# Gated mix of an FFT filter and a GELU unit on Trainium2: first loads through SyncE, last down products in single PSUM banks, other buffers and addresses for the GELU products

## The chip, the core and the metric

The kernel runs on one core of a Trainium2 chip. A core has a matrix engine (TensorE, PE in the profile; its weight loads are PEld), VectorE (DVE), ScalarE (ACT), GpSimd (POOL) and SyncE (SP), which here only issues transfers. Each engine works through its own instructions in the order in which they were recorded and waits on semaphores for what other engines and transfers produce. PE multiplies from on-chip memory (SBUF, 128 partitions) and writes into eight accumulation banks (PSUM), which DVE and ACT read. Transfers are issued by SP, POOL or ACT and carried by 16 DMA engines.

The metric is the device time of one execution in microseconds (us). Three executions of the kernel before took 1328.35 to 1328.8 us, with a median of 1328.49 us.

## What is computed

For x of 2048 tokens by 576 features, the kernel mixes a filter in frequency space with a GELU-gated unit, token by token:

```python
g = sigmoid((x * gate_w).sum(-1, keepdims=True))
X = rfft2(x, axes=(-2, -1)) * (w_r + 1j * w_i)
a = irfft2(X, s=(2048, 576), axes=(-2, -1))
b = (gelu(x @ w_gate, approximate=True) * (x @ w_up)) @ w_down     # 576 -> 4608 -> 576
return g * a + (1 - g) * b
```

## The kernel before, in words

**The gated unit fills PE.** The 4608 hidden features are 36 tiles of 128. Tokens are taken in two halves `p` of 1024, each in two blocks `tb` of 512. Every fp32 operand is split into a high and a low part (`xhi`/`xlo`, two halves of a `gub` or `dn` buffer), and a product is made of three: high by high, low by high, high by low. Hidden tiles come in pairs `i`. The first pairs of a half are made directly (`normal`, `chain`, lines L851 to L868), the rest in blocks of seven products instead of eight (`products`, `seven`, L1283 to L1389). Each pair leaves four results of 128x512, named `c11`, `c12` for block 0 and `c21`, `c22` for block 1. `finish` applies the GELU on ACT and multiplies on DVE, and `split_h` writes the result, split in two, to a hidden buffer that `take(wants)` picks from those free. From there the result is the stationary operand of the down products.

**The down products.** `down` (L958) makes a tile of 128 tokens by 576 outputs: for each of two hidden tiles (`part` 0 and 1) six products of 288 columns into a pair of PSUM banks (`ps_dn`, two such pairs in turn). ACT evicts it, scaled by 1 - g, into one of four buffers `stg`, and POOL adds that to `yd` in HBM. A block of `products` puts eight such tiles between its seven products.

**The hidden buffers.** Four of them, `base` = `hb0`, `hb1`, `hb2`, `hx`, serve the direct pairs and `c11`, `c12`; two more, `extra` = the second half of a `gub` buffer and `ext`, serve `c21`, `c22`. A buffer has 4096 bytes in a partition. Tiles are laid out in SBUF one after the other in the order in which `mk` names them, so a wider tile moves all that are named after it. In the built program the byte addresses, modulo 512, are: `hb0`, `hb1`, `hb2` and `ext` 448, the half of `gub` 384, `hx` 480, and `rows` (which also holds the operands of the column transform) 480. All `dn` buffers are at 384.

**The filter** is worked in the gaps between matmuls: DVE and ACT do the transforms along the rows, and PE does the column transform as 32 small products (`product`, L294) that stand between the others in the middle of the run.

**The start** (L1434 to L1471). `x0[k]` are the five tiles of x for the first 512 tokens, 256 KB each; `w0[:, k]` and `w1[:, k]` are the matching pieces of the first two gate/up weight tiles, 128 KB each. SP issues all of x and the weights of k = 0, POOL the other eight weight pieces. PE first does six idle products on a zeroed buffer, then `first_chains` (L870): for k = 0, 1, 2 six products for tile 0 and six for tile 1, then k = 4 and 3 of tile 0, then of tile 1. ACT makes the high part of each weight and x piece, DVE the low part, in the fixed order in which the loop records them. A transfer of SP takes one of eight semaphores in turn, and waits until the transfer eight places ahead of it has landed.

**The end** (`finale`, L1419). The last results are added and stored straight to y: four tiles with a whole pair of banks each, then four tiles whose part 0 is done for all of them before part 1. Of these, two sit in bank pairs (`pair()`), one in the two banks `px`, one in the two banks `pgu`. `down_last` (L999) makes the products, lets DVE add the tile to what was loaded (L1008, 576 columns for a whole tile, 288 for each half otherwise), and lets SP store it (L1012 or L1010).

Of the kernel before, what the change touches and what calls it, by code (L numbers as in the profile page):

```python
# [11 lines left out]
F32R = mybir.dt.float32r  # L12
# [7 lines left out]
KF = D // 2 + 1  # L20
# [3 lines left out]
HD = D // 2  # L24
KT = 5
TB = 512
SW = 2 * (KF + 1)
ROWS = 5120
UNIT = ROWS // 4
# [120 lines left out]
def _block_of_token():  # L150

    out = [0] * 16
    for o in range(16):
        out[4 * LEFT[o % 4] + LEFT[o // 4]] = o
    return out, [4 * TAKEN[o % 4] + TAKEN[o // 4] for o in out]
# [20 lines left out]
def _build(nc, tc, a):  # L176
    with ExitStack() as ctx:
# [3 lines left out]
        vec, act, pl, pe = nc.vector, nc.scalar, nc.gpsimd, nc.tensor  # L181

        def mk(n, shape, dt=F32):
            return pool.tile([P] + shape, dt, name=n, tag=n)

        def f(x):
            return x.bitcast(F32)
# [7 lines left out]
        _, loc = _block_of_token()  # L195
# [4 lines left out]
        low = mk("low", [5008])  # L200
        ext = mk("ext", [2 * TB])
        raw = [low[:, i * (KT * 256 + D):(i + 1) * (KT * 256 + D)] for i in range(2)]
        hb = [mk(f"hb{i}", [2, TB], F32R) for i in range(3)]
        gl = [mk(f"gl{i}", [TB]) for i in range(2)]
        xraw = mk("xraw", [4, TB])
        stg = [mk(f"stg{i}", [2, HD]) for i in range(4)]
        tmp = mk("tmp", [2 * UNIT + 112])
        sgn = tmp[:, 2 * UNIT + 112 - KF:]
        gs = mk("gs", [NB])
        gate = mk("gate", [NB])  # L210
        omg = mk("omg", [NB])
        msk = mk("msk", [2 + 96])
# [10 lines left out]
        def ps_gu():  # L223
            return psum.tile([P, TB], F32, name="pgu", tag="pgu", bufs=2)

        def ps_dn():
            return psum.tile([P, 2, 512], F32, name="pdn", tag="pdn", bufs=2)

        def ps_x(c):
            return psum.tile([P, TB], F32, name=f"px{c}", tag=f"px{c}", bufs=1)  # L230
# [3 lines left out]
        def ps_one():  # L234
            ones[0] += 1
            return ps_x(ones[0] % 2)

        def copy(o, i):
            act.activation(o, i, AF.Copy)  # L239
# [229 lines left out]
        def gu_at(j):  # L469
            return (j + (2 * FIRST[0] - 1) * (j >= NT)) % 3  # L470

        BLOCKS = []
        for p in range(2):
            y, z = (gu_at(NT * p + 2 * FIRST[p] - q) for q in (2, 1))
# [321 lines left out]
        def gu_of(j):  # L796
            return gub[gu_at(j)].rearrange("p (l t k) -> p l t k", l=2, t=KT)
# [13 lines left out]
        def seq(key, *steps):  # L811

            q = todo[key] = [fn for _, fn in steps]
            for n, _ in steps:
                at(n, lambda: q and q.pop(0)())
# [96 lines left out]
        base = list(hb) + [mk("hx", [2, TB], F32R)]  # L912
        extra = []
# [7 lines left out]
        def split_h(g, hold, wants=(), soon=False):  # L921

            def high():
                hold.append(take(wants))
                copy(hold[0][:, 0], g)

            def low():
                vec.tensor_tensor(hold[0][:, 1], g, f(hold[0][:, 0]), ALU.subtract)
                credit[0] -= 0.7

            return ((1, high), (2, low)) if soon else ((3, high), (5, low))

        def down_mm(ps, prev, t, part, apart=False):
            c = slice(t * P, (t + 1) * P)
            j, hold, key = prev[3][part]
            due(key)
            h = hold[0]
            due(("dn", j))
            d = dn[j % 4]
            steps = [(n, half) for n in range(3) for half in range(2)]  # L940
            for n, half in sorted(steps, key=lambda x: x[1]) if apart else steps:
                l, q = ((0, 0), (0, 1), (1, 0))[n]
                pe.matmul(ps[half], h[:, l, c], d[:, q, half * HD:(half + 1) * HD],  # L943
                          start=part == 0 and n == 0, stop=part == 1 and n == 2)
            tick(6 * 0.131)
# [44 lines left out]
        def rest(i):  # L990
            if i < 4:
                return stg[i].rearrange("p c k -> p (c k)")
            return low[:, D * (i - 4):D * (i - 3)]

        def load_last(tb):
            for i in range(4 * tb, 4 * tb + 4):
                nc.sync.dma_start(rest(i), yd[8 + i])

        def down_last(prev, t, v, part):  # L999

            i = 4 * prev[2] + t
            whole = len(v) == 1
            down_mm((v[0][:, 0, 0:HD], v[0][:, 1, 0:HD]) if whole else v, prev, t, part, not whole)
            if part == 1:
                o = rest(i).rearrange("p (c k) -> p c k", c=2)
                for c in range(1 if whole else 2):
                    oc, vc = (o, v[0][:, :, 0:HD]) if whole else (o[:, c], v[c])
                    vec.scalar_tensor_tensor(oc, vc, omg[:, 8 + i:9 + i], oc, op0=ALU.mult, op1=ALU.add)  # L1008
                    if not whole:
                        nc.sync.dma_start(a["y"][8 + i][:, c * HD:(c + 1) * HD], o[:, c])  # L1010
                if whole:
                    nc.sync.dma_start(a["y"][8 + i], rest(i))  # L1012

        def pair():
            return (ps_dn(),)
# [282 lines left out]
        def products(b, i):  # L1298

            p, j = b.p, b.p * NT + 2 * i  # L1300
# [4 lines left out]
            def finish(name, x, o):  # L1305
                g, v = x
                hold = made[name] = []

                def mult():
                    vec.tensor_tensor(o, o, v, ALU.mult)  # L1310
                    credit[0] -= 0.69

                def gelu():
                    act.activation(o, g, AF.Gelu_apprx_tanh)

                wants = extra if name in ("c21", "c22") else base
                if end and p and name in ("c21", "c12"):
                    gelu()
                    seq((name, p, i), (1, mult), *split_h(o, hold, wants, True))
                else:  # L1320
                    soon = 0 if end else 1
                    high, low = (fn for _, fn in split_h(o, hold, wants))
                    late = name in ("c22", "c12") and not (end and p)
                    seq((name, p, i), (1 + late, gelu), (2 + (soon if name != "c21" else 0) + late, mult), (4 + soon + late - end, high), (5 + 2 * soon + late, low))
# [16 lines left out]
            for n, (name, nd) in enumerate(zip(("a11", "a12", "s2", "s3", "s1", "a22", "s4"), downs)):  # L1341
# [6 lines left out]
                if n in (4, 5):  # L1348
                    w, x = dn[(j + n - 4) % 4], b.wdr[n - 4]
# [15 lines left out]
                ps = acc if n in (2, 3, 5) else fore  # L1365
# [7 lines left out]
                if n in (1, 4, 5, 6):  # L1373
                    finish(*{1: ("c11", fore, gl[0]), 4: ("c22", u3, u3[0]), 5: ("c21", acc, gl[1]), 6: ("c12", u, u[0])}[n])
# [44 lines left out]
        def finale(pend):  # L1419
            load_last(0)  # L1420
            for d, t in pend[:4]:
                v = pair()
                for part in range(2):
                    down_last(d, t, v, part)
                gap()
            d = pend[4][0]
            ps = [pair(), pair(), [ps_one()[:, 0:HD] for _ in range(2)], [ps_gu()[:, 0:HD] for _ in range(2)]]
            for part in range(2):
                for t in range(4):
                    down_last(d, t, ps[t], part)  # L1430
# [3 lines left out]
        x0 = [til[i // 9][:, TB * (i % 9):TB * (i % 9 + 1)] for i in range(2 * KT)]  # L1434
        w0, w1 = (raw[j][:, 0:KT * 256].rearrange("p (t k) -> p t k", t=KT) for j in range(2))
        w0d, w1d = (a["wgu"][j].rearrange("p (t k) -> p t k", t=KT) for j in range(2))
        for k in (0, 1, 2, 4, 3):
            nc.sync.dma_start(x0[k], a["xt"][0][:, k, 0:TB])
            (pl if k else nc.sync).dma_start(w0[:, k], w0d[:, k])
            (pl if k else nc.sync).dma_start(w1[:, k], w1d[:, k])  # L1440
        nc.sync.dma_start(msk, a["msk"])
        for k in range(KT):
            nc.sync.dma_start(x0[5 + k], a["xt"][0][:, k, TB:2 * TB])
        for i in range(2):
# [6 lines left out]
        idle = hb[2][:, 0]  # L1451
# [4 lines left out]
        ps = ps_gu()  # L1456
        for _ in range(6):
            pe.matmul(ps, idle[:, 0:P], idle, start=True, stop=True)
        for k in (0, 1, 2, 4, 3):
            for j, w in ((0, w0), (1, w1)):  # L1460
                g = gu_of(j)
                copy(g[:, 0, k], w[:, k])
                if j == 0 and k == 0:
                    vec.tensor_copy(xhi[0][:, k], x0[k])
                vec.tensor_tensor(g[:, 1, k], w[:, k], f(g[:, 0, k]), ALU.subtract)
                if j == 0 and 0 < k < 4:
                    copy(xhi[0][:, k], x0[k])
                if j == 0 and k < 4:
                    vec.tensor_tensor(xlo[0][:, k], x0[k], f(xhi[0][:, k]), ALU.subtract)
                elif j == 0:  # L1470
                    prep_x(0, k, x0[k])  # L1471
# [150 lines left out]
```

## Time and profile before

| | |
|---|---|
| median of three runs | 1328.49 us |
| the profiled execution: its own time / its span | 1328.51 / 1326.7 us |
| busy in the span | PE 1319.0, DVE 1162.4, ACT 871.7, POOL 275.6 us |
| granted clock of TensorE | 1.0 throughout |
| DMA | 247.57 MB, mean 187 GB/s, 353 GB/s in the first of 40 slices |

The span runs from the first to the last instruction; 1.8 us of the execution lie outside it. A busy PE is not a PE at its peak, since the ends of matmuls are modelled: what a product costs is read from the distance between starts, or from the chain of waits, which follows the work that ended last back from the end and gives each group the time by which it moved the end on.

### The profile page before, as it was taken

The numbers are of one execution on the slowest core, as the hardware profiler recorded it, in microseconds if no ns is written. First come the engines' busy times: TensorE is split into PE (matmuls) and PEld (weight loads), VectorE is DVE, ScalarE is ACT, GpSimd is POOL, SyncE is SP. The second block draws the span as 40 slices with busy tenths as digits, with TensorE's granted clock in tenths as the row PEclk, the third lists the DMA queues.
The fourth block names the chain that finished last, engine by engine and source line by source line (L and its number), as shares of the span: only waits on it lengthen the run. The fifth ranks groups of instructions, "written<-read, shape, count | busy, mean of one in ns | idle before, by whom it ended". The sixth has DMA issues, their size and how long they took to land.

```text
span 1326.7 us, 20231 instructions
## 1 busy us (share of the span) xinstructions
PE 1319.0 (99%) x7294; PEld 1166.8 (88%) x7294; DVE 1162.4 (88%) x1653; ACT 871.7 (66%) x1583; POOL 275.6 (21%) x350
## 2 busy tenths in 40 slices
PE   9999999999999999999999999999999999999998
PEld 7888888888888888888888988888888888888897
DVE  7789999978999997976899889799999879999844
ACT  5686765665657556787688888547665686666562
POOL 1011121221212112122302231211222232222331
PEclk9999999999999999999999999999999999999999
DMA  9346777797777777999989998787777897776896
GB/s 353 137 115 128 130 136 136 156 267 164 149 154 137 152 155 183 273 240 283 283 262 235 220 217 195 124 282 190 152 151 147 201 240 153 141 138 126 190 191 176
DMA packets 108693, 247.57 MB, mean 187 GB/s; under 512 B 12848, under 2 KB 17840, under 8 KB 106800
## 3 DMA queue, kind: packets, MB, share of 16 engines
q0 software_dynamic: 46752, 97.34, 45.8%
q1 hardware_dynamic: 61840, 148.93, 34.1%
q8 instruction: 57, 0.93, 0.3%
q14 instruction: 44, 0.36, 0.1%
HBM read 133.88 MB, written 109.95 MB: 184 GB/s over the span
## 4 chain that ended last, share of the span: by engine, by line
PE 94%; issue 3%; DMA 1%; ACT 1%; DVE 1%; POOL 1%; SPq 0%; DVEq 0%; POOLq 0%; ACTq 0%
PE pdn L943 33%; PE pgu L1290 20%; PE px L1290 20%; PE pgu L1292 3%; PE px L1292 3%; PE pgu L859 2%; PE pgu L860 2%; PE pgu L861 2%; PE px L859 1%; PE px L860 1%; PE px L861 1%; PE pdn L304 1%; PE px L304 1%; PE pgu L865 1%; PE pgu L866 1%
## 5 line engine op out<-in xcount | busy, mean ns | idle before, releaser
L956 POOL DMA_DIRECT2D yd<-stg x264 | 226.6, 865 | 941.2 <-ACT stg L975 861.8
L975 ACT ACTIVATE stg<-pdn,omg 128x576 f32<-128x576 f32 x276 | 204.6, 742 | 327.6 <-PE pdn L943 201.9
L943 PE MATMUL pdn<-dn,hb 128*128 128x288 f32 x1572 | 230.9, 294 | 0.1
L943 PEld LDWEIGHTS pdn<-dn,hb 128*128 128x128 f32 x1572 | 221.7, 188 | 9.3 <-ACT stg L975 0.4
L1277 DVE TENSOR_TENSOR gub<-low,gub 128x768 fp32r<-128x768 f32 x124 | 118.0, 952 | 9.6 <-ACT gub L1274 7.0
L1290 PE MATMUL pgu<-xhi,gub 128*128 128x512 f32 x392 | 121.9, 392 | 0.0
L239 ACT ACTIVATE gub<-low 128x512 fp32r<-128x512 f32 (+2 forms) x147 | 97.7, 666 | 19.9 <-DVE low L1267 13.6
L1290 PE MATMUL pgu<-til,gub 128*128 128x512 f32 x420 | 107.5, 391 | 0.0
L943 PE MATMUL pdn<-dn,ext 128*128 128x288 f32 x672 | 106.7, 294 | 0.0
L943 PE MATMUL pdn<-dn,gub 128*128 128x288 f32 x672 | 106.5, 294 | 0.0
L943 PEld LDWEIGHTS pdn<-dn,ext 128*128 128x128 f32 x672 | 98.0, 188 | 4.1
L943 PEld LDWEIGHTS pdn<-dn,gub 128*128 128x128 f32 x672 | 97.9, 188 | 4.0
L1290 PEld LDWEIGHTS pgu<-til,gub 128*128 128x128 f32 x420 | 76.9, 188 | 14.7 <-DVE gub L1277 0.3
L1290 PE MATMUL px<-xhi,gub 128*128 128x512 f32 x280 | 86.9, 392 | 0.0
L1290 PE MATMUL px<-til,gub 128*128 128x512 f32 x336 | 86.0, 391 | 0.0
L943 PE MATMUL pdn<-dn,hx 128*128 128x288 f32 x516 | 82.3, 296 | 0.0
L1290 PEld LDWEIGHTS pgu<-xhi,gub 128*128 128x128 f32 x392 | 70.9, 188 | 12.3
L1267 DVE TENSOR_TENSOR low<-low 128x768 f32<-128x768 f32 x81 | 77.2, 953 | 0.8
L1290 PE MATMUL pgu<-xlo,gub 128*128 128x512 f32 x196 | 76.4, 390 | 0.0
L859 PE MATMUL pgu<-xhi,gub 128*128 128x512 f32 x188 | 73.6, 391 | 0.0
L860 PE MATMUL pgu<-xhi,gub 128*128 128x512 f32 x188 | 73.4, 391 | 0.0
L861 PE MATMUL pgu<-xlo,gub 128*128 128x512 f32 x188 | 73.4, 390 | 0.0
(278 smaller groups left out, 2967.6 us busy)
## 6 DMA issues: line engine op xcount, KB each, us to landing
yd<-stg POOLq DMA_DIRECT2D x264, 288.0 KB, 5.0
low<-ws SPq DMA_DIRECT2D x94, 384.0 KB, 4.9
gub<-wd SPq DMA_DIRECT2D x56, 288.0 KB, 3.9
low<-wgu SPq DMA_DIRECT2D x13, 640.0 KB, 7.3
rows<-col POOLq DMA_DIRECT2D x32, 256.0 KB, 6.3
gub<-ws SPq DMA_DIRECT2D x18, 384.0 KB, 5.8
lo<-dn SPq DMA_DIRECT2D x18, 288.0 KB, 2.9
dn<-lo POOLq DMA_DIRECT2D x18, 288.0 KB, 5.3
```

What stands on the lines that cost most here:

```text
L239: act.activation(o, i, AF.Copy)
L304: pe.matmul(v[al][:, :NK], c[:, al, q], two(x)[:, al], start=n == 0, stop=n == 2)
L859: pe.matmul(ps, w[:, 0, k, c], xhi[tb][:, k], start=k == 0, stop=False)
L860: pe.matmul(ps, w[:, 1, k, c], xhi[tb][:, k], start=False, stop=False)
L861: pe.matmul(ps, w[:, 0, k, c], xlo[tb][:, k], start=False, stop=False)
L943: pe.matmul(ps[half], h[:, l, c], d[:, q, half * HD:(half + 1) * HD], start=part == 0 and n == 0, stop=part == 1 and n == 2)
L956: pl.dma_start(yd[u], o, accum_op=ALU.add)
L975: at(n, lambda: put(u, lambda o: act.activation(o.rearrange("p (c k) -> p c k", c=2), v[:, :, 0:HD], AF.Copy, scale=omg[:, u:u + 1]), i == 0))
L1267: vec.tensor_tensor(o, p, q, ALU.subtract)
L1277: vec.tensor_tensor(w[:, 0:5:2], x, f(w[:, 1:4]), ALU.subtract)
L1290: pe.matmul(ps, l, x[:, t], start=first and t == 0 and q == 0, stop=False, skip_group_check=True)
L1292: pe.matmul(ps, w[:, 512 + P * s:512 + P * (s + 1)], xt, start=False, stop=True, skip_group_check=True)
```

## The change

Four edits. (1) At the start SP issues x and the weights of k = 0, 1, 2 in the order in which PE needs them, with `x0[4]` before the last weight piece and `x0[3]` last; POOL issues the weight pieces of k = 4 and 3 alone, and only after it has cleared 16 columns of the buffer that the six idle products read, which makes it wait for those products. (2) In `finale` the four last tiles change places: first the one in `px`, then `pgu`, then a whole bank pair, then a bank pair used as two single banks, each half evicted and stored by itself. Where a tile is stored in halves, the second half is stored by ACT instead of SP. (3) `hb1` is widened by 448 bytes ahead of its data and named after `hb2`, and `tmp` loses 32 bytes, which moves `hb1`, `hx`, `rows` and others; `hb0`, `hb2` and `ext` are then at 448 modulo 512, `hb1`, `hx`, `rows` and the half of `gub` at 384. (4) `c21` always asks for `ext` and `c22` for the half of `gub`, where both took the first free one.

```diff
-        hb = [mk(f"hb{i}", [2, TB], F32R) for i in range(3)]
+        hb = [mk("hb0", [2, TB], F32R), None, mk("hb2", [2, TB], F32R)]
+        hb[1] = mk("hb1", [2 * TB + 112], F32R)[:, 112:].rearrange("p (l k) -> p l k", l=2)
...
-        tmp = mk("tmp", [2 * UNIT + 112])
-        sgn = tmp[:, 2 * UNIT + 112 - KF:]
+        tmp = mk("tmp", [2 * UNIT + 104])
+        sgn = tmp[:, 2 * UNIT + 104 - KF:]
...
-                        nc.sync.dma_start(a["y"][8 + i][:, c * HD:(c + 1) * HD], o[:, c])
+                        (act if c else nc.sync).dma_start(a["y"][8 + i][:, c * HD:(c + 1) * HD], o[:, c])
...
-                wants = extra if name in ("c21", "c22") else base
+                wants = dict(c21=extra[1:], c22=extra[:1]).get(name, base)
...
-            ps = [pair(), pair(), [ps_one()[:, 0:HD] for _ in range(2)], [ps_gu()[:, 0:HD] for _ in range(2)]]
+            ps = [[ps_one()[:, 0:HD] for _ in range(2)], [ps_gu()[:, 0:HD] for _ in range(2)], pair()]
+            v = ps_dn()
+            ps.append([v[:, c, 0:HD] for c in range(2)])
...
-        for k in (0, 1, 2, 4, 3):
+        for k in (0, 1, 2, 3):
             nc.sync.dma_start(x0[k], a["xt"][0][:, k, 0:TB])
-            (pl if k else nc.sync).dma_start(w0[:, k], w0d[:, k])
-            (pl if k else nc.sync).dma_start(w1[:, k], w1d[:, k])
-        nc.sync.dma_start(msk, a["msk"])
+            if k < 3:
+                nc.sync.dma_start(w0[:, k], w0d[:, k])
+            if k == 2:
+                nc.sync.dma_start(x0[4], a["xt"][0][:, 4, 0:TB])
+            if k < 3:
+                nc.sync.dma_start(w1[:, k], w1d[:, k])
+            if k == 2:
+                nc.sync.dma_start(msk, a["msk"])
...
+        pl.memset(f(idle)[:, 0:16], 0.0)
+        for w, wd, k in ((w0, w0d, 4), (w0, w0d, 3), (w1, w1d, 4), (w1, w1d, 3)):
+            pl.dma_start(w[:, k], wd[:, k])
```

The order on SP at the start of the program, before (`til` holds x, `low` the raw weights):

```order
L1438 DMA til_69<-xt 128x512
L1439 DMA low<-wgu 128x256
L1440 DMA low<-wgu 128x256
L1438 DMA til_69<-xt 128x512 x4
L1441 DMA msk<-msk 128x98
L1443 DMA til_69<-xt 128x512 x4
```

and with the change (lines of the changed kernel, here and below):

```order
L1441 DMA til_69<-xt 128x512
L1443 DMA low<-wgu 128x256
L1447 DMA low<-wgu 128x256
L1441 DMA til_69<-xt 128x512
L1443 DMA low<-wgu 128x256
L1447 DMA low<-wgu 128x256
L1441 DMA til_69<-xt 128x512
L1443 DMA low<-wgu 128x256
L1445 DMA til_69<-xt 128x512
L1447 DMA low<-wgu 128x256
L1449 DMA msk<-msk 128x98
L1441 DMA til_69<-xt 128x512
```

Four weight pieces moved from POOL's order into SP's, each ahead of the x tile of the next k. The orders of ACT, DVE and PE in this place are unchanged.

On PE, in every second block of `products`, two down tiles before (`gub2` at 384, `ext` at 448; `dn` is the moving operand):

```order
L943 MATMUL pdn_3274<-dn2_77,gub2_73 128x288 x6
L943 MATMUL pdn_3274<-dn3_78,ext_868 128x288 x6
L1290 MATMUL px0_3164<-til1_315,slot_74 128x512 x6
L1292 MATMUL px0_3164<-til0_316,slot_74 128x512
L1290 MATMUL px1_3165<-til1_315,slot_74 128x512 x6
```

and with the change:

```order
L944 MATMUL pdn_3275<-dn2_77,ext_869 128x288 x6
L944 MATMUL pdn_3275<-dn3_78,gub2_73 128x288 x6
L1291 MATMUL px0_3165<-til1_316,slot_74 128x512 x6
L1293 MATMUL px0_3165<-til0_317,slot_74 128x512
L1291 MATMUL px1_3166<-til1_316,slot_74 128x512 x6
```

The two buffers changed places in half of the blocks; nothing moved between instructions.

At the end of PE's order, before:

```order
L943 MATMUL pdn<-dn_78,ext 128x288 x6
L943 MATMUL pdn<-dn_77,hb_83 128x288 x12
L943 MATMUL px_11987<-dn_77,hb_83 128x288 x3
L943 MATMUL px_11988<-dn_77,hb_83 128x288 x3
L943 MATMUL pgu<-dn_77,hb_83 128x288 x6
L943 MATMUL pdn<-dn_78,hx 128x288 x12
L943 MATMUL px_11987<-dn_78,hx 128x288 x3
L943 MATMUL px_11988<-dn_78,hx 128x288 x3
L943 MATMUL pgu<-dn_78,hx 128x288 x6
```

and with the change:

```order
L944 MATMUL pdn<-dn_78,gub_72 128x288 x6
L944 MATMUL px_11986<-dn_77,hb_82 128x288 x3
L944 MATMUL px_11987<-dn_77,hb_82 128x288 x3
L944 MATMUL pgu<-dn_77,hb_82 128x288 x6
L944 MATMUL pdn<-dn_77,hb_82 128x288 x12
L944 MATMUL px_11986<-dn_78,hx 128x288 x3
L944 MATMUL px_11987<-dn_78,hx 128x288 x3
L944 MATMUL pgu<-dn_78,hx 128x288 x6
L944 MATMUL pdn<-dn_78,hx 128x288 x12
```

The products into bank pairs (`pdn`) moved behind those into `px` and `pgu`, in both parts.

## The prediction, made before the changed kernel ran

> **What bounds the kernel now.** I read the page first, then the chain of waits at both ends and in the middle, then the engines in order of time where the chain leaves PE.
>
> ```profile
> span 1326.7 us, 20231 instructions
> ...
> PE 94%; issue 3%; DMA 1%; ACT 1%; DVE 1%; POOL 1%; SPq 0%; DVEq 0%; POOLq 0%; ACTq 0%
> ```
>
> The end is set by PE's own work. An edit can help only where PE stands still, or by making its products closer to each other. It stands still mostly at the two ends. The chain at the start (start, us, what):
>
> ```profile
> 2.12 6.12 DMA til<-xt
> ...
> 8.27 0.64 ACT xhi L239
> ...
> 8.95 1.66 PE px L879 x6
> 10.61 1.36 PE pgu L879 x6
> ```
>
> PE waits for the second tile of x, landed at 2.12 + 6.12 = 8.24 us, and then for ACT's copy of it. From 10.61 on six products take 1.36 us and nothing interrupts them. In order of time (start, us, engine, line, what, and in brackets the idle time before and what ended it):
>
> ```profile
> 1.65 0.43 SPq L1440 DMA_DIRECT2D low<-wgu  x1
> 2.12 1.86 SPq L1438 DMA_DIRECT2D til<-xt  x4
> ...
> 5.71 0.61 PE L879 MATMUL px<-xlo,gub 128*128 128x512 f32 x2
> ...
> 6.28 0.72 ACT L239 ACTIVATE gub<-low 128x256 fp32r<-128x256 f32 x2 [2.01 <-DMA low<-wgu]
> ...
> 6.75 1.19 PE L879 MATMUL pgu<-xhi,gub 128*128 128x512 f32 x4 [0.43 <-ACT gub L239]
> ...
> 7.78 0.63 PE L879 MATMUL pgu<-xlo,gub 128*128 128x512 f32 x2
> ```
>
> **The start, edit 1.** Fed products begin 0.227 us apart (1.36 / 6). The first group's last two begin at 5.71, so a next group could begin at 5.71 + 0.45 = 6.16. It begins at 6.75, since ACT began only at 6.28 on a weight piece that SP had issued at 1.65 and waited 2.01 us for it. That is 0.59 us. This second group lasts 7.78 + 0.45 - 6.75 = 1.48, 0.12 more than 1.36. Then PE waits from 8.23 to 8.95, 0.72, and the restarted group loses another 0.12. All in all 1.55 us, which is all that can be won before 10.61; what PE loses before 5.71 is untouched.
>
> Do the data come in time now? Rates of the transfers (last column, GB/s):
>
> ```profile
> 2.00:3.00 1.00, 1.00 (x4) 0.76 (x3) 0.00 (x0) 0.22 (x2) 1.00 (x2) 1.00 0.80 262
> 3.00:4.00 1.00, 1.00 (x4) 0.56 (x2) 0.43 (x1) 0.14 (x1) 1.00 (x3) 1.00 0.99 245
> 4.00:5.00 1.00, 1.00 (x3) 0.58 (x3) 0.69 (x2) 0.27 (x1) 1.00 (x3) 1.00 0.63 151
> 5.00:6.00 1.00, 1.00 (x6) 0.77 (x4) 0.33 (x1) 0.00 (x0) 1.00 (x3) 1.00 0.82 285
> 6.00:7.00 1.00, 0.57 (x3) 0.25 (x2) 0.27 (x1) 0.72 (x2) 0.28 (x1) 1.00 0.95 356
> ```
>
> By 6.0 us 0.94 MB have moved and by 7.0 us 1.3 MB, enough for both k = 0 and k = 1 (1.05 MB) if they came in that order; now they share the engines with POOL's pieces for k = 2 to 4. In the new order and at no better rate, the second x tile (bytes 0.52 to 0.79 MB) lands at about 5.4 and the second weights by 6.3. PE wants them at 6.16 + 1.36 = 7.5, and ACT needs about 1 us before (0.36 for a weight piece, half of the 0.72 above, and 0.64 for x): 6.5. It fits. SP's issues do not hold it up: 0.43 to 0.47 us for each transfer, so the second x tile leaves at 2.12 as now and the eighth transfer is issued by 4.4. POOL's four pieces begin after the idle products, at about 4.5 us; its pieces now land in 6.7 us (median, first row below), so the last, issued by about 6.5, lands by 13.2. PE reaches k = 4 of tile 0 at 6.16 + 5 x 1.36 = 13.0, k = 3 of it at 13.9 and those of tile 1 at 15.2 and 16.1, and each piece is wanted about 1 us sooner. This cover is thin, since ACT's order has tile 1's k = 4 piece, due at 12.5, ahead of tile 0's k = 3.
>
> ```profile
> low<-wgu POOLq DMA_DIRECT2D x8, 128.0 KB, 6.7
> ...
> 50.00:60.00 10.00, 10.00 (x59) 8.94 (x58) 6.30 (x11) 6.13 (x11) 0.00 (x0) 1.00 0.50 182
> ```
>
> I take 1.55 us, with bounds 0 and 1.7. It is not lost later: DVE's gate sums may wait some tenths for `rows`, but no product waits for them soon, and from 50 to 60 us DVE is busy 6.30 of 10 us (second row; the columns after the window are its length and the busy time of PE, PEld, DVE, ACT, POOL), so it catches up.
>
> The Trainium skill, DMA: Bandwidth & Descriptors, "Issuing engines are not separate DMA queues", says that transfers from any engine run on the same 16 DMA engines and that another issuer saves only the time to issue. By it the move to SP wins no rate; the rows above show that the order alone would do, and where it didn't the time would be that of the first rival.
>
> **The products, edits 3 and 4.** Two down tiles one behind the other are 24 products (pieces of the chain at four places):
>
> ```profile
> 28.74 3.17 PE pdn L943 x24
> ...
> 169.44 3.18 PE pdn L943 x24
> ...
> 634.73 3.17 PE pdn L943 x24
> ...
> 1280.48 3.16 PE pdn L943 x24
> ```
>
> By the program's order the first is from `hb0` and `hb1` (448 and 448), the second from `hb2` and `hx` (448, 480), the third from `gub` and `ext` (384, 448), the fourth from `ext` and `gub` (448, 384). The differences are small but the same at all other pairs. With the change all 284 tiles have 448 and then 384. Per tile that is 5 ns for 88 tiles of the first kind, 10 ns for 84 of the second, 5 ns for 56 of the third: 0.44 + 0.84 + 0.28 = 1.56 us at most. Tiles that stand alone read 1.58 us in all kinds, so they differ by less; I take 1.2, with bounds 0 (the steps are those of the rounding) and 1.6.
>
> The column products have their stationary operand in `rows`, which goes from 480 to 384 like `hx`:
>
> ```profile
> L943 PE MATMUL pdn<-dn,hb 128*128 128x288 f32 x1572 | 230.9, 294 | 0.1
> L943 PE MATMUL pdn<-dn,hx 128*128 128x288 f32 x516 | 82.3, 296 | 0.0
> L304 PE MATMUL px<-rows 128*128 128x290 f32 x96 | 15.7, 298 | 0.1
> L304 PE MATMUL pdn<-rows 128*128 128x290 f32 x96 | 15.6, 298 | 0.6 <-ACT stg L975 0.6
> ```
>
> They take 298 ns where 288 columns take 294, and two more columns explain one. Half of the rest, 1.5 ns on 192 products, is 0.3 us (0 to 0.6).
>
> **The end, edit 2 and the ACT stores.** The chain there:
>
> ```profile
> 1315.56 0.83 DVE low L1008
> ...
> 1316.43 1.06 PE pdn L943 x6
> 1317.50 0.79 PE px L943 x6
> 1318.29 0.80 PE pgu L943 x6
> 1319.08 1.61 PE pdn L943 x12
> ```
>
> PE's second part-0 group waits for DVE to empty the bank pair. With `px` and `pgu` first, the pairs are asked for 1.6 us later, at about 1317.0 and 1317.7, while DVE leaves the last at 1315.56 + 0.83 = 1316.4. The stall and its restart go: the twelve products take 1317.33 - 1315.36 = 1.97 us to the next group (rows below) instead of 0.79 + 0.80, so 0.38. What is late next is DVE:
>
> ```profile
> 1315.36 2.13 PE L943 MATMUL pdn<-dn,hb 128*128 128x288 f32 x12
> 1317.33 0.95 PE L943 MATMUL px<-dn,hb 128*128 128x288 f32 x6
> 1322.31 0.93 DVE L1008 SCALAR_TENSOR_TENSOR stg<-pgu,omg,stg 128x288 f32<-128x288 f32 x2
> ```
>
> Let part 1 begin at S (1319.08). Now DVE ends its last half at 1322.31 + 0.93 = S + 4.16. In the new order two half-tiles follow PE, the whole tile is ready at S + 2.45 and takes about 0.8, and the last tile's halves both wait for all of its products (S + 3.25) and take 0.93: S + 4.18. Nothing is won on DVE.
>
> ```profile
> L1010 SPq DMA_DIRECT2D y<-stg x4: 388/406/413, 1322.0 to 1323.5; - x4
> DMA to landing us min/median/max: 1.9/2.0/2.1
> L1611 SPq EVENT_SEMAPHORE  x11: 17/28/28, 1323.9 to 1326.7; - x11
> L1611 SPq DRAIN  x3: 7/7/7, 1325.9 to 1326.2; - x3
> ```
>
> SP issues the four half stores one behind the other, the last at 1323.5, 0.26 after DVE ended. ACT has nothing else to do there and can issue almost at once: 0.2. The store lands 1.9 later, at 1325.4; SP then walks through its eight transfer semaphores until 1325.9, since the last store holds the first of them. In the new program the last store holds the sixth: two or three steps instead of eight, 0.3 us less. The end gives 0.38 + 0.2 + 0.3 = 0.9 (0.3 to 1.0; an ACT store that starts slowly, which no row shows, would take from it).
>
> **The sum**: 1.55 + 1.2 + 0.3 + 0.9 = 3.95 us. The profiled execution took 1328.51, 0.02 above the median, so 1328.51 - 3.95 = 1324.6 us, with a span of about 1322.8.
>
> **Rivals.** *POOL's late pieces, or the order alone, give the start back.* For it: the thin cover, and 151 GB/s in the fifth microsecond with both issuers at work. Against it: POOL's pieces have some 6 us or more between issue and need. Price 1.55: 1326.1, with 0.16. *The addresses buy nothing*, the 0.01 us belonging to the place of a pair in its block. For it: the size of the steps. Against it: `hx` alone is at 296 ns among its like. Price 1.5: 1326.1, with 0.11. (The Trainium skill, SBUF — State Buffer, "Operand start alignment", asks only that a start be a multiple of the element size, as a matter of legality and not of speed; a reader of it alone would give the addresses no price, and the time of this rival.) *Slower: the column products wait for their banks.* They share the bank pairs with the down tiles, and two of the sixteen into `pdn` (96 products, six each) now wait for ACT's eviction:
>
> ```profile
> PE pdn L304 <- ACT stg L975: 0.6, 2, 0.4
> ```
>
> Should the new phase between PE and ACT make all sixteen wait as the longer one does, 0.4 us and about 0.1 for the restart, that is 16 x 0.5 = 8 us: 1324.6 + 8 = 1332, with 0.07. It decides where ACT ends an eviction after PE has come to that pair. Against it: ACT is fed by PE there and moves with it. That the buffers aren't taken as asked is excluded by the order of the built program: all tiles stand as named.
>
> **Chances.** Forecast 0.65, the rivals as given, 0.01 for else. A change of 0.2% (2.7 us) is about what a measurement tells from none: faster means under 1325.8. The forecast is that, the first two rivals are the same, the third slower: 0.65, 0.27, 0.08. The range is 1323.5 to 1326.9: all upper bounds together (1.7 + 1.6 + 0.6 + 1.0) give 1323.6; its top holds the start at nothing with the end at its lower bound (1324.6 + 1.55 + 0.6), and either of the first two rivals. The slower case and both rivals at once are left out.
>
> **What would show it.** Right: on PE no gap between 6.2 and 17.6 us and the first L860 product at about 17.5; pairs of tiles at 3.16 everywhere; no wait for DVE among the last groups, the last store on ACT some 0.05 us after DVE, and the span's end within 1.2 us of its landing. Wrong: ACT waiting for `low` after 9 us with PE behind it; pairs still at 3.17 and 3.18; new stalls on `pdn` at 640 to 830 us.

## The result, and the profile after

| | before | with the change |
|---|---|---|
| median of 21 executions each | 1328.55 us | 1326.01 us |
| their range | 1327.79 to 1329.28 us | 1325.59 to 1328.17 us |
| ratio, with its 95% interval | | 0.9982 (0.9975 to 0.9988) |
| the profiled execution: own time / span | 1328.51 / 1326.7 us | 1326.14 / 1324.4 us |

The change takes 2.5 us off the time, 0.19%. The forecast was 1324.6 us, 1.4 too little; the range of 1323.5 to 1326.9 held it. By the time alone the first two rivals, at 1326.1 each, are nearer than the forecast; it is the profiles that tell them apart. The profile after, first its heading and the new queue, which carries ACT's stores (packets, MB, share of 16 engines):

```profile
span 1324.4 us, 20236 instructions
...
q10 hardware_dynamic: 432, 0.44, 0.1%
```

**The start.** The chain of waits (start, us, what):

```profile
4.38 2.75 PE px L880 x6
7.14 1.57 PE pgu L880 x6
8.71 1.36 PE px L880 x6
10.07 1.36 PE pgu L880 x6
...
18.68 0.23 PE px L860
```

The chain before reached the same product here:

```profile
19.22 0.23 PE px L859
```

No transfer and no ACT copy stands in the chain any more: PE works through. Yet it reaches L860 at 18.68, where the chain before had 19.22 (L859 there): 0.54 won, not 1.55. (The chain counts from the modelled end of the product before; the products themselves begin at 18.52 and 19.06, and from here on it is such starts that are given.) PE's timeline says why (start, us, engine, line, what, and in brackets the idle time before):

```profile
1.46 2.93 PE L1466 MATMUL pgu<-hb 128*128 128x512 f32 x6 [1.46 <-DVE gate L1462]
4.21 2.07 PE L880 MATMUL px<-xhi,gub 128*128 128x512 f32 x4
6.08 1.05 PE L880 MATMUL px<-xlo,gub 128*128 128x512 f32 x2
6.93 1.32 PE L880 MATMUL pgu<-xhi,gub 128*128 128x512 f32 x4
8.09 0.62 PE L880 MATMUL pgu<-xlo,gub 128*128 128x512 f32 x2
8.54 1.07 PE L880 MATMUL px<-xhi,gub 128*128 128x512 f32 x4
```

The two products at 6.08 begin (6.93 - 6.08) / 2 = 0.425 us apart, the two at 8.09 only (8.54 - 8.09) / 2 = 0.225. Nothing waited; PE ran at half its clock. The trace's record of the granted clock goes to full at 7.42 us here and at 5.11 us in the profile before. The page rounds this away in its slices of 33 us.

**The products.** Pairs of down tiles, at the same four places of the chain as before:

```profile
28.20 3.16 PE pdn L944 x24
...
168.80 3.16 PE pdn L944 x24
...
633.55 3.16 PE pdn L944 x24
...
1278.94 3.16 PE pdn L944 x24
```

All four now read 3.16. In the groups by form (count, busy us, mean ns) `hx` has come down from 296 to 294, but the column products have not come down with it, they take 300 and 298 where both took 298:

```profile
L944 PE MATMUL pdn<-dn,hb 128*128 128x288 f32 x1572 | 230.2, 294 | 0.0
...
L944 PE MATMUL pdn<-dn,hx 128*128 128x288 f32 x516 | 81.7, 294 | 0.0
...
L305 PE MATMUL pdn<-rows 128*128 128x290 f32 x96 | 15.8, 300 | 0.5 <-ACT stg L976 0.5
L305 PE MATMUL px<-rows 128*128 128x290 f32 x96 | 15.8, 298 | 0.1
```

**The end**, again from the chain:

```profile
1313.96 0.80 PE px L944 x6
1314.76 0.80 PE pgu L944 x6
1315.56 1.59 PE pdn L944 x12
1317.15 0.80 PE px L944 x6
1317.94 0.80 PE pgu L944 x6
1318.74 1.61 PE pdn L944 x12
1320.35 0.03 issue
1320.38 0.52 DVE stg L1009
```

DVE's `low` of 0.83 us, which stood among PE's groups before, is gone from it; every group follows the one before in 0.80 for six. Behind it ACT issues the last store, and SP's drain (the instruction behind its last wait) comes at 1323.5 (duration in ns, first and last start):

```profile
L1011 ACTq DMA_DIRECT2D y<-stg x3: 338/338/382, 1318.6 to 1321.4; - x3
L1622 SPq DRAIN  x3: 7/7/7, 1323.5 to 1323.8; - x3
```

**Where the time went.** The distance of PE's starts, product by product, gives the time between marks that are the same in both programs. Differences to the profile before, in us; *start* ends with the first product of the main chains (L859 before, L860 after), *middle* is the stretch with the column products, *tail* is what follows the last product:

```
run      start   to 627 us   middle   to 1312 us   last 59   tail    clock full at
after    -0.54     -0.64     +0.27      -0.64       -0.40    -0.40        7.42
again    -1.50     -0.59     +0.26      -0.64       -0.40    -0.40        4.85
again2   -0.98     -0.59     +0.28      -0.64       -0.40    -0.40        6.31
head     -1.40     +0.04     +0.03       0.00        0.00    -0.23        4.49
tail     +0.05     +0.05     +0.05       0.00       -0.39    -0.12        6.04
addr     -0.38     -0.59     +0.29      -0.61       -0.04    -0.07        4.32
rows     +0.50     -0.59     +0.20      -0.51       -0.40    -0.41        4.73
walk     -1.12     -0.63     +0.30      -0.64       -0.40    -0.53        5.90
slip     -1.37     -0.60     +0.32      -0.64       -0.40    -0.10        5.54
```

The first row is the change, the others are the runs told of below. Behind the start the parts of *after*, *again* and *again2*, one program, repeat to about 0.05 us, and the parts add up; the start alone differs from execution to execution. Each row is one execution.

The two stretches of down tiles gain more than the down products do. Counted by the product that begins each distance, of the 1.28 us of *after* the down products have 0.75, the products of the blocks of seven 0.59, and the direct ones give back 0.07; *again* has 0.72, 0.58 and 0.08. The operands of the block's products (`xhi`, `xlo`, `til`, `gub`, `slot`) are named ahead of `hb1` and did not move. Two thirds of their gain stands on the first seven products behind a down tile, so part of it may be the down tiles' own, ending late; that is not shown.

### The profile page after: what moved, and what is told of

Same layout as the page of the kernel before. It is cut to its first block, busy times and chain, and to the rows that moved or that the text cites. A ratio compares the mean times of both kernels' runs of the same rounds, so it can differ in the third digit from the quotient of the medians.

```text
span 1324.4 us, 20236 instructions
## 1 busy us (share of the span) xinstructions
PE 1318.2 (100%) x7294; PEld 1166.9 (88%) x7294; DVE 1163.1 (88%) x1654; ACT 871.9 (66%) x1583; POOL 273.4 (21%) x347
## 4 chain that ended last, share of the span: by engine, by line
PE 96%; DVE 1%; ACT 1%; DMA 1%; issue 0%; SPq 0%; DVEq 0%; ACTq 0%
PE pdn L944 33%; PE pgu L1291 20%; PE px L1291 20%; PE pgu L1293 3%; PE px L1293 3%; PE pgu L860 3%; PE pgu L861 3%; PE pgu L862 3%; PE px L860 1%; PE px L861 1%; PE px L862 1%; PE pdn L305 1%; PE px L305 1%; PE pgu L866 1%; PE pgu L867 1%; PE px L880 1%
## 5 line engine op out<-in xcount | busy, mean ns | idle before, releaser
L944 PEld LDWEIGHTS pdn<-dn,ext 128*128 128x128 f32 x672 | 100.8, 188 | 8.0
L944 PEld LDWEIGHTS pdn<-dn,gub 128*128 128x128 f32 x672 | 95.0, 188 | 0.0
L861 PE MATMUL pgu<-xhi,gub 128*128 128x512 f32 x188 | 73.7, 392 | 0.0
L860 PE MATMUL pgu<-xhi,gub 128*128 128x512 f32 x188 | 73.7, 392 | 0.0
```

The costliest lines, as they stand in the source:

```text
L860: pe.matmul(ps, w[:, 0, k, c], xhi[tb][:, k], start=k == 0, stop=False)
L861: pe.matmul(ps, w[:, 1, k, c], xhi[tb][:, k], start=False, stop=False)
```

## The experiments

### The edits one at a time

*head* is the kernel before with the start's loads alone (edit 1), *tail* with the last four tiles and ACT's stores alone (edit 2), *addr* with the addresses and buffers alone (edits 3 and 4). Their edits are the pieces of the change's diff above.

> The kernel before with edit 1 alone (order and issuers of the first loads). Theory of the prediction: the data stalls were the whole cost of the start, 1.55 us less than before. Theory formed after the changed kernel's profile (clock): with the stalls gone PE does its first fed products 427 ns apart, not 227, until the granted clock goes up, and when that comes sets the gain: 0.55 us less than before where it comes at 7.4 us as in the profile after, up to 1.7 where it comes at 5.1 as in the profile before. The records of this run show the moment, and the first L859 product stands at 18.5 for a late one and at 17.4 for an early one.

> The kernel before with edit 2 alone (order of the last four tiles, second halves stored by ACT). Theory: 0.8 us less than before (0.4 on PE, 0.4 behind the last product), by the profile after. Rival: the end gains only on PE, 0.4. Its start is that of the kernel before, so it is also a second look at when the clock goes up there: 5.1 us again if the program sets it, another time if it differs by execution.

> The kernel before with edits 3 and 4 alone (addresses, and which buffer c21 and c22 take). Theory: down tiles 1.28 us less, column products 0.3 more, together 1.0 less. Prediction: 1.5 less. Rival (the differences belong to the place in the block and not to the addresses): 0. A third look at the start of the kernel before.

Against 1328.72 us before, the medians of 11 executions were 1327.21 (head), 1328.16 (tail) and 1327.68 (addr): 1.5, 0.6 and 1.0 less, together 3.1. The 95% intervals of these ratios reach some 0.0009 (1.2 us) to either side, so only that of *head* stays clear of 1, and barely; what each part is worth is read from the traces.

- *head*: the clock went up at 4.49 us, PE reached the main chains at 17.66, 1.40 sooner than in the profile before. With an early clock the start gives nearly all that was forecast. It also shortened the tail by 0.23 us, which nobody had expected of an edit at the start.
- *tail*: PE's stall went, 0.39, but the tail gave only 0.12. The theory's 0.4 behind the last product fell for edit 2 alone; the rival's 0.4 in all is nearer to the 0.5 of this profile.
- *addr*: 0.59 and 0.61 less in the two stretches of down tiles, 0.29 more in the middle. That the addresses buy nothing is refuted; that they buy something in the middle too is as well: there the down products win 0.19 and the others lose more.

All of these keep a start from which PE works without a pause of more than 0.2 us until after 4.3 us, and the clock goes up at 5.11, 6.04 and 4.32 us in three executions with the loads of before.

### The same kernel again

*again* and *again2* are the changed kernel, unchanged.

> The changed kernel once more, unchanged. Theory (the clock goes up at a time that differs by execution, and sets the start): the records show another moment than 7.4 us, anywhere from 4.3 to 8.3, and the first L860 product stands at 17.6 + about half of what that moment is later than 4.5 us (18.52 at 7.4); everything behind it is as in the profile after to some 0.05 us. Rival (the program sets the moment): 7.4 us and 18.5 again.

> The changed kernel, unchanged, a third time, beside the three that follow. Theory (the clock's moment differs by execution): another moment than 7.4 and 4.85 us, between 4.3 and 8.3; the first product of L860 at 17.6 plus half of what the moment is later than 4.5 us, unless a load comes late; all behind it as in the first profile after to 0.05 us. Rival: one of the two moments already seen.

The clock went up at 4.85 and at 6.31 us, so the program does not set the moment. In *again*, PE's timeline:

```profile
4.28 1.45 PE L880 MATMUL px<-xhi,gub 128*128 128x512 f32 x4
5.56 0.62 PE L880 MATMUL px<-xlo,gub 128*128 128x512 f32 x2
6.03 1.09 PE L880 MATMUL pgu<-xhi,gub 128*128 128x512 f32 x4
...
17.56 0.39 PE L860 MATMUL px<-xhi,gub 128*128 128x512 f32 x1
```

Here the fed products begin 0.23 us apart after the first, and L860 begins at 17.56: as the prediction would have it ("about 17.5"), and 1.50 less than before. The five profiles of this start that are compared here, in all of which the loads came in time, are the three of the changed kernel and *walk* and *slip* below; *rows*, with a late load, is left out. Ordered by the clock they reach L860 at 17.56 (4.85), 17.69 (5.54), 17.94 (5.90), 18.07 (6.31) and 18.52 (7.42). From 5.54 to 7.42 that is 0.83 / 1.88 = 0.44 us lost for each us that the clock is late; two rates of 0.425 and 0.225 would lose 1 - 0.225 / 0.425 = 0.47. The mean gain of the five is 1.10 us.

The medians, 1325.59 and 1325.57 us (10 executions each, ratios 0.9978, 0.9969 to 0.9987, to 1328.61 and 1328.45), are some 0.4 us better than the 1326.01 of the first 21. A moment earlier by 1 us on the mean would account for that. The executions of *head*, *again* and *again2* ran on three different chips; what shifts the mean was not tried.

### What decides when the clock goes up

*idle1* leaves one idle product of the six; *early* lets them start sooner.

```diff
-        for _ in range(6):
+        for _ in range(1):
             pe.matmul(ps, idle[:, 0:P], idle, start=True, stop=True)
-        pl.memset(f(idle)[:, 0:16], 0.0)
...
+                if j == 0 and k == 0:
+                    pl.memset(w[:, 0, 0:16], 0.0)
...
```

> The changed kernel with one idle product at the start instead of six, and POOL's four loads released by the first weight piece being split, about when they were. PE then has nothing to do from 1.9 to 4.2 us. If the clock goes up at the end of a period of 3.4 us in which PE worked throughout (periods that end at 4.0, 7.4, 10.8 us in the profile after), it goes up at 10.8: 1.7 us more than the changed kernel. If it goes up some 6 us after PE began to work without a break: at 10.1, 1.3 us more. If the moment has nothing to do with PE's work: at 7.4 and no more time than the changed kernel.

*idle1*'s PE:

```profile
1.46 0.80 PE L1466 MATMUL pgu<-hb 128*128 128x512 f32 x1 [1.46 <-DVE gate L1462]
4.35 2.07 PE L880 MATMUL px<-xhi,gub 128*128 128x512 f32 x4 [2.10 <-ACT gub L240]
6.22 1.05 PE L880 MATMUL px<-xlo,gub 128*128 128x512 f32 x2
7.07 1.52 PE L880 MATMUL pgu<-xhi,gub 128*128 128x512 f32 x4
8.42 0.63 PE L880 MATMUL pgu<-xlo,gub 128*128 128x512 f32 x2
```

The clock went up at 8.00 us, which none of the three theories had named. The median was 1327.12, 1.6 less than the 1328.72 before it, where the changed kernel gains 2.5 to 3.0: the idle products are worth some 0.9 to 1.4 us. POOL's loads left 0.36 us later here than in the profile after, but behind 4.35 us no product of this profile waits for a load. So the moment seems to depend on PE's work, by this one profile and the median. The first theory had taken the ends of the periods from the profile after. With their ends left free it is not refuted: a period of 3.41 us that ends at 8.00 begins at 4.59, and PE works all through it.

```diff
-        vec.memset(f(idle), 0.0)
+        vec.memset(f(idle)[:, 0:P], 0.0)
...
-        for _ in range(6):
-            pe.matmul(ps, idle[:, 0:P], idle, start=True, stop=True)
+        for _ in range(7):
+            pe.matmul(ps.rearrange("p (a k) -> p a k", a=4), idle[:, 0:P],
+                      idle[:, 0:P].unsqueeze(1).to_broadcast([P, 4, P]), start=True, stop=True)
```

> The changed kernel with only the first 128 of 512 columns of the idle buffer cleared (the idle products read these four times over) and seven idle products instead of six. PE then starts 0.35 us sooner, at about 1.1 us, with the first fed product where it was. If the clock goes up a fixed or at least some time after PE began to work, it does so 0.35 us sooner on the mean, and the time is about 0.15 us less than the changed kernel's; if its moment has nothing to do with PE's start: no difference.

PE began at 1.06 us, the clock went up at 6.02, and the median was 1325.83 us beside 1325.59 for *again* on the same chip. No gain is seen. One of 0.15 us would be less than such medians tell apart, so this is inconclusive.

Counted from PE's first product after its last long idle time (1.46 us, 1.06 in *early*, 4.35 in *idle1*), the fourteen profiles have the clock full after 2.9 us (*addr*) to 6.0 us (*after*), and *idle1*, 3.65 us after its second beginning, fits in.

The traces show a period. In every one of the fourteen the record of the full clock lasts either 1317.545 or 1320.958 us, which is 386 or 387 times 3.41333: it begins and ends on the beat of one period, and only the phase differs. The period that ends with the clock up began between 0.91 (*addr*) and 4.59 us (*idle1*). In the profile after, the period before it, from 0.59 to 4.00, did not raise the clock, though PE worked in it from 1.46 on; in *addr*, work from 1.46 to 4.32 was enough.

The Trainium skill, TensorE: Matmul & The Clock Gate, section "What's actually happening", says that the clock is raised by how busy PE was in windows of some 3.4 us that run on regardless of the program. The period of the traces and a spread of 3.1 us between executions agree with windows that run freely. It also says that the point varies by 500 ns either way; here it is three times that.

### The very first load through ACT

```diff
             if k < 3:
-                nc.sync.dma_start(w0[:, k], w0d[:, k])
+                (nc.sync if k else act).dma_start(w0[:, k], w0d[:, k])
```

> The changed kernel with the very first weight piece issued by ACT, ahead of its table load, instead of second by SP. The first fed product waits for that piece and then for ACT's copy of it: 0.4 us sooner, at 3.85 instead of 4.21 us, and all other SP loads leave 0.43 us sooner. Theory (after the change the start is bound by PE and its clock, no longer by the order of the loads): 0.2 to 0.4 us less than the changed kernel. Rival (the DMA engines are full at the start, so an earlier issue lands no sooner): no difference.

The median was 1326.10 us against 1325.59 for *again*: no gain, if anything a loss. The piece was issued at 0.74 us instead of 1.19, and PE got it later, in order of time:

```profile
0.74 0.41 ACTq L1443 DMA_DIRECT2D low<-wgu  x1
1.18 1.28 ACT L1463 ACT_TABLE_LOAD   x1 [1.18 <-PEq L1619]
2.47 0.20 ACT L1463 ACTIVATE gate<-gate 128x1 f32<-128x1 f32 x1
4.32 0.72 ACT L240 ACTIVATE gub<-low 128x256 fp32r<-128x256 f32 x2 [1.64 <-DMA low<-wgu]
```

It landed at 4.29, not at 3.72 as in the profile after, and the first x tile, issued at 0.74 as there, at 4.11, not at 3.38: three transfers now left within 0.45 us where two had, and all three landed by 4.49. So in this one profile the earlier issue did not make the piece land earlier; that sharing is the cause is argued, not shown. The Trainium skill, DMA: Bandwidth & Descriptors, "Issuing engines are not separate DMA queues", says that transfers of all issuers run on the same DMA engines, and this trace agrees.

### The column products' addresses

*rows* puts `hx` behind `hb1` and widens `tmp`, so that only `rows` and what is named behind it go back to 480.

```diff
+        hx = mk("hx", [2, TB], F32R)
...
-        tmp = mk("tmp", [2 * UNIT + 104])
+        tmp = mk("tmp", [2 * UNIT + 128])
...
```

> The changed kernel with hx named ahead of gl0 and tmp 96 bytes wider, so that only rows (and what is named behind it) goes back to 480 modulo 512, and all operands of the down products stay where the change put them. Theory (the column products' part of the change is its addresses in rows): the stretch with the column products, 0.27 us longer after than before, goes back by 0.2 to 0.3, and the down products keep their 1.28: some 0.25 us less than the changed kernel. Rival (the stretch is longer for its new phase between engines): no difference.

The distance of starts in the middle stretch, against before, by what kind of product begins it (us; waits apart):

```
            column   gate/up   down    waits    sum
after       +0.16    +0.36    -0.18    -0.07   +0.27
again       +0.16    +0.36    -0.19    -0.07   +0.26
rows         0.00    +0.13    -0.20    +0.27   +0.20
```

The column products go back to where they were, as the theory had it, and so do 0.23 us of the gate/up products between them, which it had not foreseen. A new gap on PE at 800.1 us, 0.29 long, eats most of it in this one profile, which names no releaser for it: the whole stretch went back by 0.07, not by 0.2 to 0.3. To 1312 us *rows* gives back another 0.13. The addresses in `rows` make the column products slower, that is shown; nearly all of the 0.16 is on the 96 products into `pdn`. None of the operands of the gate/up products moved; what makes them slower stays open. The time is no better: its median was 1325.56 us, *again*'s 1325.59.

This profile is also the prediction's first rival at work, in one execution. Its clock went up early, at 4.73, yet PE reached L861 (L860 after) only at 19.56:

```profile
10.14 0.61 PE L881 MATMUL pgu<-xlo,gub 128*128 128x512 f32 x2
11.94 1.21 PE L881 MATMUL px<-xhi,gub 128*128 128x512 f32 x4 [1.19 <-ACT xhi L241]
```

and its chain names the load:

```profile
4.02 6.91 DMA low<-wgu
10.93 0.02 issue
10.96 0.42 ACT gub L241
11.37 0.53 ACT xhi L241
```

SP's weight piece for k = 2 landed at 10.93; in the profile after it was there at 8.06. This execution took 1327.28 us, the most of that run's eleven.

### POOL's pieces later

*later* releases POOL's four loads by a later event, so that they do not share the engines with SP's.

```diff
-        pl.memset(f(idle)[:, 0:16], 0.0)
...
+                if j == 1 and k == 0:
+                    pl.memset(w[:, 0, 0:16], 0.0)
...
```

> The changed kernel with POOL's four loads released by the split of the second weight piece (about 6.3 us) instead of by the idle products (4.4 us). Theory (late loads of k = 2 in some executions come from sharing the DMA engines with POOL's pieces): SP's loads of k = 2 land sooner, no stall for them in the profile, and the median is the changed kernel's or up to 0.3 us less, with fewer executions above 1326.5. Rival (the first one of the prediction: POOL's pieces then come too late for k = 4 and 3): stalls of some tenths at 12 to 16 us, up to 1 us more.

The rival had it: 1326.77 us, 1.2 more than *again2* beside it. From its chain, and below it PE's two waits:

```profile
7.42 6.36 DMA low<-wgu
13.78 0.02 issue
13.80 0.73 ACT gub L240 x2
14.53 0.53 ACT xhi L240
...
13.67 1.17 PE L880 MATMUL px<-xtl,gub 128*128 128x512 f32 x4 [0.38 <-DVE xtl L245]
15.10 1.19 PE L880 MATMUL px<-xhi,gub 128*128 128x512 f32 x4 [0.27 <-ACT xhi L240]
```

POOL's third piece, issued at 7.42, lands at 13.78, and ACT's copy for the product at 15.10 stands behind it. The product at 13.67 waits for a copy that came after POOL's first piece, landed at 11.25. SP's last piece for k = 2 did land sooner, at 9.24 where *slip* had 9.65, as the theory had it, but no product had waited for it there either. PE reaches L860 at 18.85 us, where *slip*, told of next and run once, had 17.69 with the clock up at about the same moment (5.54 against 5.42). The cover of POOL's pieces, which the prediction called thin, ends within the 1.7 us by which this moved them.

### The walk through the semaphores

At the end SP waits for its transfers' semaphores one after the other, in a fixed order. *walk* splits one load into three transfers, *slip* into four, which turns the eight semaphores on by two and three places.

```diff
-            nc.sync.dma_start(raw[i][:, KT * 256:], a["wd"][i])
+            for c in range(0, D, D // 3 if i else D):
+                e = c + (D // 3 if i else D)
+                nc.sync.dma_start(raw[i][:, KT * 256 + c:KT * 256 + e], a["wd"][i][:, c:e])
```

> The changed kernel with the second load of wd split into three transfers of SP, which turns the eight semaphores of the transfers by two places: the last store to y then holds the last of those that SP walks through at the end, not the third from last. Theory (each semaphore behind that of the last store costs a step of 0.06 us): 0.12 us less behind the last product than the changed kernel, 4.20 instead of 4.32. Rival (the walk is hidden): 4.32.

> As the run before, with four transfers instead of three: the last store then holds the first of the eight semaphores, as in the kernel before. Theory (the steps of the walk): seven steps instead of two behind the landing, 0.3 us more than the changed kernel behind the last product, 4.62. Rival (ACT issuing the last store is what shortened the end): 4.32.

From the traces, one execution each, in us: from the last product's start to DVE's end, to the last store's issue, to its landing, to SP's drain (with the semaphores stepped through after the landing), and to the end:

```
          to DVE   to issue      to landing   walk          to end   sum
before     1.24    0.23 (SP)       1.92       0.51 (8)       0.82    4.72
head       1.24    0.23 (SP)       1.92       0.26 (4)       0.83    4.49
tail       1.28    0.08 (ACT)      1.98       0.45 (7)       0.82    4.60
after      1.28    0.08 (ACT)      1.95       0.20 (3)       0.82    4.32
walk       1.27    0.08 (ACT)      1.94       0.08 (1)       0.82    4.19
slip       1.27    0.08 (ACT)      1.94       0.51 (8)       0.83    4.62
```

Both came out as expected: 4.19 for 4.20, 4.62 for 4.62. The walk was shortened not by ACT's stores but by the four transfers that edit 1 moved to SP at the other end of the program; *head* has most of that gain without edit 2 (four steps instead of eight), *tail* has one step. *walk* is the fastest version by its mechanism, 0.13 us; the medians (1325.61 us, *again2* 1325.57) cannot show so little.

## Why the prediction was right in part

- **Start, 1.55 us.** The step that failed is "the first group's last two begin at 5.71, so a next group could begin at 5.71 + 0.45 = 6.16", with "what PE loses before 5.71 is untouched". It took the first group from one execution in which the clock happened to be up at 5.11 us. The rows it quoted held the warning: four products took 1.54 us there, and 1.19 in the group behind. With the stalls gone, what PE does until the clock is up is fed work at half speed, and that lasted until 4.85, 6.31 and 7.42 us. The gain is 0.54 to 1.50 us, 1.10 on the mean of five profiles. The kernel before hides a late clock, since PE waits for data later anyway: 19.06 at 5.11 and 19.11 at 6.04 (in *addr* 18.68, as the second x tile had landed at 7.87, not at 8.24). No gap on PE from 6.2 to 17.6 us came true, but the product expected at 17.5 began at 18.52. The bounds of 0 and 1.7 held the gain, but the lower one stood for late data; that it also covers a late clock is luck.
- **Products, 1.2 us.** Right in that the addresses and buffers win, as *addr* shows, and near in size by luck. It priced the down tiles alone. The down products won 0.75 outside the middle and 0.18 in it, some 0.9; the other 0.6 of the 1.23 to 1.28 outside the middle stands on the block's products between them, for which there was no term.
- **Column products, 0.3 us won.** Wrong in sign. It priced the place of the stationary operand alone; both operands lie in `rows` and both moved. The column products lost 0.16, and gate/up products between them, whose operands did not move, 0.36, the second without a cause that the runs show.
- **End, 0.9 us.** 0.80: PE's stall 0.39 (0.38 forecast), ACT's issue 0.15 (0.2), the walk 0.31 (0.3); DVE and the landing give back 0.03 each. The last two rows of the table above show the walk apart from ACT's stores, which the prediction had tied together.

The sum by the first profile: 0.54 + 1.28 - 0.27 + 0.80 = 2.35, the difference of the spans (1326.7 and 1324.4). With the mean start it is 2.9 us, near the 2.5 to 3.0 of the three comparisons.

**The rivals.** POOL's pieces or the loads give the start back: not in any profile of the changed kernel, but SP's load did in that of *rows*, where it cost 2.0 us (19.56 against *again*'s 17.56), and POOL's pieces in *later*, 1.2 us; the price given was 1.55. The addresses buy nothing: refuted by *addr*. Both rivals stood at 1326.1, and the first median of 1326.01 would have fitted either; the start fell short for a reason that was no rival, the clock. The change was to come out under 1325.8: the first median did not, those of *again* and *again2* did. Column products waiting for ACT: their waits changed by less than 0.1 us.

## What to carry to other kernels

Before a stall at the start is priced, ask at what clock the work behind it will run: read the distance of the first products' starts, look at more than one execution, and count only what is left when the clock comes late. When operands are moved to better addresses, list every operand in the moved tile and measure each kind of product, those whose operands stay too; those not meant can lose what the others win. A transfer more or less on a queue shifts which semaphore the last store holds, which is worth up to 0.43 us here, far from the edit.

## What the hardware showed that was not expected

The granted clock of the matrix engine goes up 2.9 to 6.0 us after PE begins to work, at another moment in each execution, and stays up for a whole number of periods of 3.4133 us (386 or 387 in the fourteen profiles). With one idle product instead of six the kernel is about 1 us slower. Operand addresses that differ by 96 bytes modulo 512 change the distance of 290-column products by about 1 ns (0.16 us over 192, as *rows* shows by putting it back), and products whose own operands did not move change with them. Issued 0.45 us earlier, the first weight piece landed 0.57 us later, in one profile.
